# Attention and expert routing in one kernel: head pairs turned on VectorE, score buffers as a ring at the start, a changed load order at the seam

## The chip, the cores and the metric

The kernel runs on one core of a Trainium2 chip. Its time is the device time in microseconds (us) of one execution; lower is better. The engines of the core work side by side, each on its own list of instructions: TensorE (PE: matrix products and transposes, results in PSUM), VectorE (DVE), ScalarE (ACT), GpSimd (POOL) and SyncE (SP), which only issues transfers (DMA). SBUF is the working memory, PSUM the small memory of 8 banks that PE writes to.

## The reference

Attention over 4 batches, 12 heads, 448 tokens of 64 values, then a mixture of 8 experts, one expert for each of the 1792 tokens:

```
scores = cap * tanh((q @ k.T) / sqrt(64) / cap)
attn   = exp(scores - rowmax);  attn /= attn.sum(-1) + 1e-9
x      = (attn @ v), heads side by side           # 1792 x 768
logits = x @ w_gate;  e = argmax(logits)
gate   = softmax(logits)[e];  eom = sigmoid(x @ w_output_gate)[e]
out    = gate * eom * (relu(x @ w1[e]) @ w2[e])   # only the chosen expert
```

## The kernel before

**Units.** A unit is one batch and two heads (p and p + 6); there are 24 (6 for each batch), numbered u. The main loop does for each u on PE: the scores (`qk`, 4 tiles: three of two PSUM banks, one of one bank, each the sum of three products of a high and a low part of q and k), then `pv` of the unit before (8 products, result `u`), and every second unit the sums of the exponentials (`sums`). ACT takes the tanh of each score tile (PSUM to SBUF, `pt`) and one exp over the whole unit. POOL adds the exponentials up for the sums (`presum`, tile `pb`). DVE makes the planes of q and k: it turns the raw tile (`turned`: 32x32 blocks, which come out right because the load has put the blocks in place), casts it to the high part and subtracts for the low part (`planes_of`). Units 0 to 2 load q and k in natural order and PE turns them (`nat_k`, `nat_q`).

**k's planes** are 512 columns: 384 keys of both heads, and 128 columns where each head has its last 64 keys and zeros in the other head's half. DVE writes the first 384 with one operation and the two blocks of 64x64 with two more, for the high and again for the low part; the zeros are set once at the start.

**Score buffers.** PSUM has one bank `t` (all turning by DVE), one bank `sm`, and the pool `ps_s`: A and B (two banks each), C and D (one each). In units 0 to 2 the tiles go A, B, A, C; tile three of a unit waits until ACT has read tile one.

**Work for the router**, for each batch while the next one's units run, is hung into slots of the loop (`at`, slots f, g, h, q, e of a unit, in this order; x = 0 is the second unit of the next batch): reciprocals of the sums, then for each pair p the row `row_tr` (four PE transposes into a PSUM tile `trow`), `row_out` (DVE times the reciprocals, into one of three tiles `xr`) and a store into the token array `xs` in DRAM by SP; beside it the logits, the choice of an expert (`choose`: many small DVE operations), each token's place in the expert's table (`rank_mm`, `place`, `enter`) and a scatter into tables in DRAM by POOL (`scatter`).

**SP's list** is in program order: loads of k, q and v some units ahead, the stores of rows (`store_rows`, at a unit's end), at the seam the tables (`fetch_dma`, tile `tc`) and the weights (`load_raw`). Each of its transfers waits on the one eight places before it (eight semaphores taken in turn). `TURN` says how many planes are made before and after the middle of a unit; planes are made about three units ahead.

**The seam.** When the last unit's `pv` is done, the first expert block starts: POOL gathers 128 rows of `xs` by the table `tc` (`gather`), PE turns them (`tx`, tile `pt_x`), and the products with the weights follow (`php`, `py`). The expert part is the rest of the time.

Of the kernel before, what the change touches and what calls it, by code (L numbers as in the profile page):

```python
# [22 lines left out]
def tile_kernel(ctx: ExitStack, tc, q, k, v, cap, w_gate, w_ogate, w1, w2, out):  # L23
# [26 lines left out]
    for i, kind in enumerate((2, 4)):  # L50
# [8 lines left out]
    TURN = {0: (0, 0), 1: (0, 0), 3: (2, 1), 5: (2, 1), 6: (2, 1), 7: (2, 1), 9: (2, 1), 10: (1, 0), 11: (1, 0), 13: (2, 1),  # L59
            14: (2, 1), 15: (2, 1), 17: (1, 0), 20: (1, 0), 21: (0, 0), 22: (0, 0)}  # L60
# [22 lines left out]
    ps_s = att.enter_context(tc.tile_pool(name="ps_s", bufs=1, space=PSUM))  # L83
# [24 lines left out]
    def load_natural(dst, src, n, m, engs):  # L108
        for j in range(2):
            engs[j].dma_start(out=dst[:, 0:n, j], in_=src[j, 0:n * m].rearrange("(c p) d -> p c d", c=n))  # L110

    def load_nat(u, engs):
        (k0, q0), k_, q_ = nat[u], heads(k, u), heads(q, u)
        load_natural(k0, k_, NK, 128, engs)
        engs[1].dma_start(out=k0[0:64, NK], in_=k_[:, SK:S].rearrange("j p d -> p j d"))
        load_natural(q0, q_, NCH, CP, engs)

    def load_pair(src, u, tiles, to):
        t = raw1[tiles[u // 2 % 3]][:, 0:2 * S].rearrange("p (h r a) -> p h r a", h=2, a=32)
# [12 lines left out]

    def load_q(u):
        load_pair(q, u, (2, 3, 5), ldq)

    def v_main(u, eng):
        load_natural(vvs[u // 2 % 2][:, u % 2], heads(v, u), NK, 128, (eng, eng))

    def v_tails(u, eng):
        for j in range(2):  # L140
            h = j * NP + u % NP
            eng.dma_start(out=vvs[u // 2 % 2][64 * j:64 * j + 64, :, NK, j],
                          in_=v[u // NP, h:h + 2, SK:S].rearrange("h p d -> p h d"))
# [43 lines left out]
    for hl in kpl:  # L187
# [145 lines left out]
    def t_k(u):  # L333
        pl[u] = planes_of(k_parts(u, turned(ldk.pop(u), S)))
# [22 lines left out]

    def scores(name, z):
        return ps_s.tile([128, 2, 512], F32, tag="AB"[z], name=name)

    def single(name, z):
        return ps_s.tile([128, 512], F32, tag="CD"[z], name=name)
# [14 lines left out]
    def nat_q(u):  # L377
        pq = (scores("tq0", 1)[:, 0] if u == 2 else single("tq0", 1))[:, 0:S]
        for c in range(NCH):
            nc.tensor.transpose(pq[:, c * CP:(c + 1) * CP], nat[u][1][:, c].rearrange("p j d -> p (j d)"), ident[0:CP, 0:CP])  # L380
        return pq

    def qk(u, s):
        KH, KL, QH, QL = pl[u]
        if s == 0:
            pt[u] = ptp.tile([128, 2 * NK + 1, S], F32, tag="pt", name="pt")
        n = 2 if s < NK else 1
        sl = slice(s * 128, (s + 1) * 128)
        if s < NK:
            ps = scores("s", s % 2)  # L390
            for i, (x, y) in enumerate(((KH, QH), (KL, QH), (KH, QL))):
                for j in range(2):
                    h = slice(64 * j, 64 * j + 64)
                    nc.tensor.matmul(ps[:, j, 0:S], lhsT=x[h, sl], rhs=y[h], start=(i == 0), stop=(i == 2))  # L394
            ps = ps[:, :, 0:S]
        else:
            ps = single("s3", 0)[:, 0:S]
# [65 lines left out]
    def end_of_batch(b):  # L463
# [21 lines left out]
        def recips():  # L485
            r = T("rec", [CP, NCH, NP // 2, 4])
            nc.vector.tensor_scalar(out=r.rearrange("p c n j -> p c j n"), in0=rt["trec"][:, :, :, 0:NP // 2],
                                    scalar1=epsc[0:CP], scalar2=None, op0=ALU.add)
            nc.vector.reciprocal(out=r, in_=r)
            rec[b] = r.rearrange("p c n j -> p c (n j)")  # L490
# [24 lines left out]
        def gate_mul(g):  # L515
            if g == 0:
                T("gm", [CP, NCH, H, 16])
            for i in range(2):
                c = 2 * g + i
                nc.vector.tensor_tensor(  # L520
                    out=rt["gm"][:, c], in0=rt["pg"][:, i].rearrange("p (h e) -> p h e", h=H),
                    in1=rec[b][:, c].unsqueeze(2).to_broadcast([CP, H, 16]), op=ALU.mult)

        def logits():
            l = T("lg", [CP, NCH, 16])
# [3 lines left out]
            d = T("d")  # L529
            nc.vector.tensor_tensor(out=d, in0=l[:, :, 0:E], in1=mx.unsqueeze(2).to_broadcast(sh), op=ALU.subtract)  # L530

        def choose():

            d = rt["d"]
            cand = T("cand")
            stt(cand, d, 0.0, ALU.is_lt, iota8[0:CP], ALU.add)
            fi = T("fi", [CP, NCH])
# [4 lines left out]
            nc.vector.tensor_tensor(out=og, in0=ohb, in1=rt["lg"][:, :, E:2 * E], op=ALU.mult)  # L542
            den = T("den", [CP, 2, NCH])
            nc.vector.tensor_reduce(out=den[:, 1], in_=og, axis=AX.X, op=ALU.add)
# [15 lines left out]
        def place():  # L560
            ohb, ps = rt["ohb"], rt["ps"]
            rk = T("rk")
# [6 lines left out]
        def place2():  # L569
            rk = rt["rk"]  # L570
            nc.vector.tensor_tensor(out=rk, in0=rk, in1=rt["ohb"], op=ALU.mult)
            nc.vector.tensor_reduce(out=posi, in_=rk, axis=AX.X, op=ALU.max)

        def enter():

            den = rt["den"]
            nc.vector.tensor_reduce(out=den[:, 0], in_=rt["ex"], axis=AX.X, op=ALU.add)
            nc.vector.tensor_scalar(out=den[:, 1], in0=den[:, 1], scalar1=1.0, scalar2=None, op0=ALU.add)
            stt(den[:, 0], den[:, 0], 1e-9, ALU.add, den[:, 1], ALU.mult)
# [19 lines left out]
        def row_out(p):  # L599
            nrow[0] += 1  # L600
            x = xrp.tile([CP, NCH, 128], F32, tag=f"xr{nrow[0] % 3}", name="xr")
# [15 lines left out]

        L = lambda *fs: (lambda: [f() for f in fs])
        P = lambda f, *a: (lambda: f(*a))
        rws = [L(P(row_tr, p), P(row_out, p)) for p in range(NP)]  # L620
# [3 lines left out]
        if b < B - 2:  # L624
            at = {(-2, "q"): [g0], (0, "q"): [g1], (0, "e"): [sums_out], (1, "g"): [t[1]],
                  (2, "g"): [rws[0], rws[1]], (3, "g"): gts, (3, "h"): [logits], (4, "g"): [rws[2], rws[3]], (4, "h"): [choose],
                  (5, "g"): [rank_mm, place, rws[4]], (5, "h"): [place2, enter], (6, "g"): [rws[5]]}
            for i, x in enumerate(((6, "g"), (8, "g"), (9, "g"), (10, "g")) if b == 0 else ((6, "g"),) * NCH):
                at.setdefault(x, []).append(P(scatter, (i,)))
        elif b == B - 2:  # L630
# [6 lines left out]
                  (2, "g"): [rws[4], rws[5]], (2, "h"): [store_rows, P(load_v, NU - 2), *[nx] * 6, P(set_known, NE)],  # L637
                  (2, "q"): [lds[0], fd[0], lds[1], fd[1]],
# [342 lines left out]
    for u in range(NU):  # L981
        if u % 2 and u < NU - 3:
            load_v(u + 1)
        spare[0] = 0
# [386 lines left out]
```

## Time and the profile before

| | |
|---|---|
| median of 3 runs | 512.97 us (510.51 to 514.29) |
| profiled execution | 508.09 us, span 506.5 us |
| granted TensorE clock, mean | 0.996 |
| busy share PE, DVE, ACT, POOL | 96%, 76%, 73%, 57% |
| unit 3 (first with planes by DVE) begins on PE | 28.64 us |
| unit 8, unit 20 begin on PE | 63.88 us, 159.13 us |
| last full `pv` in the attention ends, first expert block begins on PE | 193.7 us, 197.62 us |

A window's row gives the busy time of each engine in it, then the granted clock, the busy share of the DMA engines and the rate; a timeline's row the start, the time from the first start to the last end of the merged instructions, the engine and line, and in brackets the engine's idle time before them and what ended it. PE's instructions overlap, so what a group costs PE is the distance to the start of the next one.

### The profile page before, as it was taken

To read this page: it belongs to the slowest core of one execution; us is meant where nothing else is said; L and a number is where in the kernel's file an instruction comes from. 1 tells how busy PE (TensorE), PEld (TensorE's weight loads), DVE (VectorE), ACT (ScalarE), POOL (GpSimd) and SP (SyncE) were. 2 spreads that over 40 slices of the span, in tenths; PEclk is the share of its full clock that TensorE was granted. 3 is DMA by queue.
4 is the path that set the end of the run, shared out by engine and by line. 5 is a ranking of instruction groups with operands and counts; after the bars stand their busy time and mean duration, and the time that the engine had idled before them with its cause. 6 is when DMAs were issued, how large, how long until landed. Compare 5 with 4: busy or idle time off the path is not lost. (4 is left out here: it accounts for less than half of the span.)

```text
span 506.5 us, 9980 instructions
## 1 busy us (share of the span) xinstructions
PE 487.3 (96%) x3064; PEld 338.1 (67%) x3064; DVE 385.3 (76%) x746; ACT 370.9 (73%) x433; POOL 290.8 (57%) x310
## 2 busy tenths in 40 slices
PE   7899999999999996999999999999999999999994
PEld 5444455444545442779988979978788867686691
DVE  5679899898998896898989869867677847565450
ACT  5899988889987794457588968867687856674551
POOL 7799998888998515575359682137363143622001
PEclk9999999999999999999999999999999999999998
DMA  7888868585531548873299245189689599790001
GB/s 174 138 151 143 143 120 148 96 148 97 83 70 38 106 122 305 273 240 116 96 384 363 72 146 207 32 289 349 224 305 379 204 396 404 200 380 33 1 33 50
DMA packets 152379, 91.92 MB, mean 181 GB/s; under 512 B 135026, under 2 KB 135162, under 8 KB 152320
## 3 DMA queue, kind: packets, MB, share of 16 engines
q1 hardware_dynamic: 142336, 58.24, 43.5%
q0 software_dynamic: 8832, 32.74, 17.6%
q8 instruction: 26, 0.43, 0.4%
q10 hardware_dynamic: 1152, 0.25, 0.2%
q14 instruction: 33, 0.27, 0.2%
HBM read 123.68 MB, written 12.04 MB: 268 GB/s over the span
## 5 line engine op out<-in xcount | busy, mean ns | idle before, releaser
L1074 DVE TENSOR_TENSOR wr<-raw,wr 128x768 fp32r<-128x768 f32 (+1 forms) x167 | 171.9, 1067 | 63.4 <-ACT wr L1073 62.0
L1073 ACT ACTIVATE wr<-raw 128x768 fp32r<-128x768 f32 (+1 forms) x167 | 150.4, 935 | 22.3 <-PE py L1095 10.3
L401 ACT ACTIVATE pt<-s,icap 128x896 f32<-128x896 f32 (+1 forms) x96 | 80.4, 916 | 12.9 <-PE s L394 12.2
L412 PE MATMUL u<-pt,vv 128*64 128x448 f32 x384 | 77.5, 545 | 0.3 <-ACT pt L404 0.3
L1095 PE MATMUL py<-wr,hh 128*128 128x384 f32 x352 | 77.3, 340 | 0.0
L1164 POOL DMA_INDIRECT out_dram<-yo,ti x13 | 20.2, 1555 | 98.7 <-ACT yo L1162 83.4
L1095 PE MATMUL php<-wr,xh 128*128 128x512 f32 x264 | 74.8, 404 | 0.0
L404 ACT ACTIVATE pt<-pt,capc 128x3136 f32<-128x3136 f32 x24 | 69.9, 2912 | 0.6
L1095 PEld LDWEIGHTS py<-wr,hh 128*128 128x128 f32 x352 | 61.2, 188 | 4.0 <-issue 3.7
L1095 PEld LDWEIGHTS php<-wr,xh 128*128 128x128 f32 x264 | 47.4, 188 | 12.8 <-issue 2.5
L412 PEld LDWEIGHTS u<-pt,vv 128*64 128x64 f32 x384 | 25.4, 136 | 39.3 <-issue 35.7
L420 POOL TENSOR_TENSOR pb<-pt 128x896 f32<-128x896 f32 x20 | 42.4, 2118 | 12.7 <-ACT pt L404 5.5
L425 POOL TENSOR_TENSOR pb<-pb,pt 64x448 f32<-64x448 f32 x40 | 45.6, 1139 | 3.1
L1095 PE MATMUL py<-wr,hl 128*128 128x384 f32 x176 | 44.8, 335 | 0.0
L421 POOL TENSOR_TENSOR pb<-pb,pt 128x896 f32<-128x896 f32 x20 | 42.0, 2102 | 1.6
L1095 PE MATMUL php<-wr,xl 128*128 128x512 f32 x132 | 41.5, 395 | 0.0
L1211 POOL DMA_DIRECT2D rh<-in_moe_w_dram x42 | 23.2, 555 | 15.8 <-DVE wr L1074 7.8
L1095 PEld LDWEIGHTS py<-wr,hl 128*128 128x128 f32 x176 | 31.8, 188 | 0.0
L1095 PEld LDWEIGHTS php<-wr,xl 128*128 128x128 f32 x132 | 24.7, 187 | 6.0
L290 DVE STREAM_TRANSPOSE tk<-raw 128x448 f32<-128x448 f32 x42 | 27.5, 655 | 0.9
L875 POOL DMA_INDIRECT xg<-xs,ti x14 | 19.3, 1381 | 6.1 <-POOL ti L868 3.7
L888 ACT ACTIVATE xh<-pt_x 128x512 fp32r<-128x512 f32 (+1 forms) x28 | 12.3, 487 | 13.3 <-PE pt_x L887 13.3
(315 smaller groups left out, 814.7 us busy)
## 6 DMA issues: line engine op xcount, KB each, us to landing
raw<-in_moe_w_dram SPq DMA_DIRECT2D x78, 512.0 KB
raw<-in_moe_w_dram SPq DMA_DIRECT2D x104, 384.0 KB
rh<-in_moe_w_dram POOLq DMA_DIRECT2D x18, 512.0 KB, 6.5
rh<-in_moe_w_dram POOLq DMA_DIRECT2D x24, 384.0 KB, 8.1
raw<-in_q_dram SPq DMA_DIRECT2D x45, 112.0 KB
vv<-in_v_dram SPq DMA_DIRECT2D x48, 96.0 KB
raw<-in_k_dram SPq DMA_DIRECT2D x40, 112.0 KB
xs<-xr SPq DMA_DIRECT2D x36, 112.0 KB
```

The costliest lines, as they stand in the source:

```text
L290: nc.vector.transpose(out=ps, in_=src.rearrange("p r a -> p (r a)"))
L401: nc.scalar.activation(out=pt[u][:, 2 * s:2 * s + n], in_=ps, func=ACTF.Tanh, scale=icap)
L404: nc.scalar.activation(out=pt[u], in_=pt[u], func=ACTF.Exp, scale=capc)
L412: nc.tensor.matmul(ups[u][64 * j:64 * j + 64], lhsT=V[:, c, j, :], rhs=P[:, 2 * c + (j if c < NK else 0)], start=(c == 0), stop=(c == NK))
L420: eng.tensor_tensor(out=s1[u], in0=P[:, 0:2], in1=P[:, 2:4], op=ALU.add)
L421: eng.tensor_tensor(out=s1[u], in0=s1[u], in1=P[:, 4:6], op=ALU.add)
L425: eng.tensor_tensor(out=s1[u][h, j], in0=s1[u][h, j], in1=P[h, 2 * NK], op=ALU.add)
L1073: nc.scalar.activation(out=t[:, 0, 0:F], in_=raw, func=ACTF.Copy)
L1074: nc.vector.tensor_tensor(out=t[:, 1, 0:F], in0=raw, in1=t[:, 0, 0:F].bitcast(F32), op=ALU.subtract)
L1095: nc.tensor.matmul(ps[g][:, 0:n], lhsT=st[:, c], rhs=w[:, z, g * n:(g + 1) * n], start=(c == 0 and st is hi and z == 0), stop=(c == (KD, K ...
L1164: nc.gpsimd.indirect_dma_start(out=out, out_offset=bass.IndirectOffsetOnAxis(ap=ti, axis=0), in_=y, in_offset=None, bounds_check=NT - 1, o ...
L1211: nc.gpsimd.dma_start(out=d, in_=rows_of(src, e, w, c), **kw)
```

## The change

**Rows of odd pairs.** For batches 0 and 1 the pairs 1, 3, 5 are no longer turned by PE: DVE turns the unit's result `ut` in blocks into PSUM (`row_v`, tile `tkr`), multiplies with reciprocals that it has turned the same way (`recips_b`, from the sums), and SP stores the row with four transfers of 32 partitions and 32 values each (128 bytes) where the two before had 64 values (256 bytes). The slots move: row 0 now follows the reciprocals in slot g of x = 1, rows 1, 3, 5 stand in slot e.

**Keys.** The zeros stand in the raw tile; a k tile is turned with two operations (384 and 128 columns), and the 512 columns are cast and subtracted at once. Each head's tile is loaded for itself: eight transfers for two units where there were four. Which 64 keys are a head's own differs between the two heads, so v's loads take other rows.

**Small tiles.** For batches 0 to 2 the logits, differences, indices, ranks and denominators stand in the bank `t` instead of SBUF; epsilon is added by ACT while it copies the sums; `gate_mul` does two blocks with one operation.

**Score buffers.** In units 0 to 2 the six banks are a ring of three tiles of two banks, for scores, natural q and `u`; unit 1's last tile takes `sm`. Before unit 3 the pool is opened again as A, B, C, D.

**Seam.** The first table is fetched before the last unit's v and before the first two weight tiles.

```diff
-    TURN = {0: (0, 0), 1: (0, 0), 3: (2, 1), 5: (2, 1), 6: (2, 1), 7: (2, 1), 9: (2, 1), 10: (1, 0), 11: (1, 0), 13: (2, 1),
-            14: (2, 1), 15: (2, 1), 17: (1, 0), 20: (1, 0), 21: (0, 0), 22: (0, 0)}
+    TURN = {0: (0, 0), 1: (0, 0), 3: (2, 1), 5: (2, 1), 6: (2, 1), 7: (2, 1), 13: (2, 1), 19: (2, 1),
+            20: (0, 0), 21: (0, 0), 22: (0, 0)}
...
+    def load_k(u):
+        t = kview[u // 2 % 3]
+        for i in range(u % 2, 2):
+            for c in range(4):
+                j, x = divmod(c, 2)
+                nc.sync.dma_start(
+                    out=t[32 * c:32 * c + 32, i, 2 * j:2 * j + 14],
+                    in_=blocks(k[u // NP, j * NP + u % NP + i - u % 2], x).rearrange("(r b) a -> b r a", b=32))
...
+    for t in kview:
+        nc.vector.memset(t[0:64, :, 14:16], 0.0)
+        nc.vector.memset(t[64:128, :, 0:2], 0.0)
...
     def turned(src, n):
         ps = tbank([128, n], "tk")
-        nc.vector.transpose(out=ps, in_=src.rearrange("p r a -> p (r a)"))
+        if n == S:
+            nc.vector.transpose(out=ps, in_=src.rearrange("p r a -> p (r a)"))
+        else:
+            nc.vector.transpose(out=ps[:, 0:SK], in_=src[:, 2:14].rearrange("p r a -> p (r a)"))
+            nc.vector.transpose(out=ps[:, SK:].rearrange("p (n k) -> p n k", n=2),
+                                in_=src.rearrange("p (n r) a -> p n (r a)", r=2)[:, 0::7])
...
     def scores(name, z):
-        return ps_s.tile([128, 2, 512], F32, tag="AB"[z], name=name)
+        ring[0] += 1
+        return ps_s[0].tile([128, 2, 512], F32, tag="AB"[z] if begun else f"r{ring[0] % 3}", name=name)
...
+    def fixed():
+        begin.close()
+        ps_s[0] = att.enter_context(tc.tile_pool(name="ps_s", reuse_waits="tile", bufs=1, space=PSUM))
...
             ssb = T("ssb", [128, S])
-            nc.scalar.activation(out=ssb, in_=smt.pop(b), func=ACTF.Copy)
+            nc.scalar.activation(out=ssb, in_=smt.pop(b), func=ACTF.Identity, bias=epsc)
...
-            rk = T("rk")
+            rk = rt["rk"] = small("rkb", sh) if b < B - 1 else T("rk")
...
+        def recips_b():
+            ps = tbank([128, S], "tks")
+            nc.vector.transpose(out=ps, in_=rt["ssb"])
...
+            for a in range(4):
+                g = 2 + a // 2
+                nc.vector.reciprocal(out=r[32 * a:32 * a + 32], in_=t[32 * g:32 * g + 32, 0:NP // 2])
+
+        def row_v(p):
+            nrow[0] += 1
+            ps = tbank([128, S], "tkr")
+            nc.vector.transpose(out=ps, in_=ut[b * NP + p])
+            x = xrp.tile([128, NCH * 128], F32, tag=f"xr{nrow[0] % 3}", name="xr")[:, 0:S].rearrange("p (t m) -> p t m", m=32)
+            nc.vector.tensor_tensor(out=x, in0=ps.rearrange("p (t m) -> p t m", m=32),
+                                    in1=rt["recb"][:, p // 2].unsqueeze(2).to_broadcast([128, NB, 32]), op=ALU.mult)
...
-            at = {(-2, "q"): [g0], (0, "q"): [g1], (0, "e"): [sums_out], (1, "g"): [t[1]],
-                  (2, "g"): [rws[0], rws[1]], (3, "g"): gts, (3, "h"): [logits], (4, "g"): [rws[2], rws[3]], (4, "h"): [choose],
-                  (5, "g"): [rank_mm, place, rws[4]], (5, "h"): [place2, enter], (6, "g"): [rws[5]]}
+            at = {(-2, "q"): [g0], (0, "q"): [g1], (0, "e"): [sums_out], (1, "g"): [t[1], rws[0]], (1, "e"): [recips_b],
+                  (2, "e"): [rws[1]], (3, "g"): gts, (3, "e"): [rws[3]], (4, "g"): [rws[2]], (4, "h"): [logits, choose],
+                  (5, "g"): [rank_mm, place, place2, rws[4]], (5, "h"): [enter], (6, "e"): [rws[5]]}
...
-                  (2, "g"): [rws[4], rws[5]], (2, "h"): [store_rows, P(load_v, NU - 2), *[nx] * 6, P(set_known, NE)],
-                  (2, "q"): [lds[0], fd[0], lds[1], fd[1]],
+                  (2, "g"): [rws[4], rws[5]], (2, "h"): [store_rows, P(v_main, NU - 2, nc.sync), P(v_tails, NU - 2, nc.sync), *[nx] * 6, P(set_known, NE)],
+                  (2, "q"): [fd[0], P(v_main, NU - 1, nc.sync), *lds[:2], fd[1]],
...
+        if u == NN:
+            fixed()
```

PE's list at the end of unit 9's scores (`s`), the rows of batch 0, `pv` (`u`) and the sums (`sm`), before:

```order
L394 MATMUL s<-QH,K4H 128x448 x2
L394 MATMUL s<-QH,K4L 128x448 x2
L394 MATMUL s<-QL,K4H 128x448 x2
L597 MATMUL trow<-ident,ut 112x128 x8
L412 MATMUL u<-pt,vv_120 64x448 x8
L444 MATMUL sm<-pb,ohc 32x448 x4
```

and now:

```order
L434 MATMUL s<-QH,K4H 128x448 x2
L434 MATMUL s<-QH,K4L 128x448 x2
L434 MATMUL s<-QL,K4H 128x448 x2
L452 MATMUL u<-pt,vv_120 64x448 x8
L484 MATMUL sm<-pb,ohc 32x448 x4
```

Eight transposes (rows 0 and 1) are gone here; row 0's four now stand one unit earlier, right behind the reciprocals' transposes `trec`. DVE's list in the same unit (planes of k, planes of q, rows), before:

```order
L290 STREAM_TRANSPOSE tk<-raw_0_106 128x448
L280 CAST K2H<-tk 128x384
L280 CAST K2H<-tk 64x64 x2
L286 TENSOR_TENSOR K2L<-tk,K2H 128x384
L286 TENSOR_TENSOR K2L<-tk,K2H 64x64 x2
L290 STREAM_TRANSPOSE tk<-raw_2_108 128x448
L280 CAST QH<-tk 128x448
L286 TENSOR_TENSOR QL<-tk,QH 128x448
L602 TENSOR_TENSOR xr<-trow,rec 112x512 x2
```

and now:

```order
L310 STREAM_TRANSPOSE tk<-raw_0_106 128x384
L311 STREAM_TRANSPOSE tk<-raw_0_106 128x128
L297 CAST K2H<-tk 128x512
L303 TENSOR_TENSOR K2L<-tk,K2H 128x512
L308 STREAM_TRANSPOSE tk<-raw_2_108 128x448
L297 CAST QH<-tk 128x448
L303 TENSOR_TENSOR QL<-tk,QH 128x448
L682 STREAM_TRANSPOSE tkr<-ut 128x448
L684 TENSOR_TENSOR xr<-tkr,recb 128x448
```

Six operations behind the turning of k (the small ones stand as x2) have become two of full width behind two turnings, and row 1 is two operations of DVE. SP's list at the seam (`vv`: v of the last two units; `tc<-tab`: pieces of the first table; `raw_0_106`: the first weight tile; TENSOR_LOAD: a number read into a register), before:

```order
L142 DMA vv_121<-in_v_dram 64x2x64 x2
L110 DMA vv_121<-in_v_dram 128x3x64 x2
L831 TENSOR_LOAD meta
L831 ISA x2
L837 ISA
L837 DMA raw_0_106<-in_moe_w_dram 128x1024
L857 TENSOR_LOAD meta
L857 ISA x2
L860 ISA
L860 DMA tc<-tab_102 128x2
```

and now:

```order
L938 DMA tc<-tab_104 128x2
L938 ISA
L938 DMA tc<-tab_105 128x2
L114 DMA vv_121<-in_v_dram 128x3x64 x2
L909 TENSOR_LOAD meta
L909 ISA x2
L915 ISA
L915 DMA raw_0_106<-in_moe_w_dram 128x1024
```

The table's four pieces (the last one stands here) have moved ahead of v's last load and of the weight tile.

## Rows read from the trace of the kernel before

**Rows 1.** Windows: stretch, length, busy us of each engine, clock, DMA share, GB/s
```profile
0.00:30.00 30.00, 24.68 (x170) 15.54 (x170) 18.65 (x88) 22.00 (x21) 22.85 (x46) 1.00 0.77 154
30.00:66.00 36.00, 36.00 (x226) 16.73 (x224) 32.34 (x73) 33.28 (x30) 33.99 (x21) 1.00 0.86 148
66.00:153.00 87.00, 86.67 (x556) 43.05 (x557) 79.64 (x186) 77.44 (x76) 77.02 (x50) 1.00 0.60 107
...
198.00:506.50 308.50, 300.48 (x1874) 243.50 (x1872) 217.43 (x305) 205.30 (x276) 131.99 (x172) 0.99 0.60 217
```

**Rows 2.** Waits of PE in 0:30: total us, times, longest
```profile
PE s L394 <- ACT pt L401: 2.7, 3, 1.7
```

**Rows 3.** Timeline of ACT in 10:200 (tanh L401, exp L404)
```profile
11.52 0.63 ACT L401 ACTIVATE pt<-s,icap 128x448 f32<-128x448 f32 x1 [0.47 <-PE s L399]
...
22.79 3.53 ACT L401 ACTIVATE pt<-s,icap 128x896 f32<-128x896 f32 x4 [1.35 <-PE s L394]
...
115.35 2.91 ACT L404 ACTIVATE pt<-pt,capc 128x3136 f32<-128x3136 f32 x1
...
122.02 2.91 ACT L404 ACTIVATE pt<-pt,capc 128x3136 f32<-128x3136 f32 x1
```

**Rows 4.** Timeline of PE, units 9, 12, 19 and 20
```profile
73.98 1.08 PE L597 MATMUL trow<-ident,ut 128*112 128x128 f32 x8
74.99 3.23 PE L412 MATMUL u<-pt,vv 128*64 128x448 f32 x16
...
98.44 0.65 PE L597 MATMUL trow<-ident,ut 128*112 128x128 f32 x4
99.02 3.23 PE L412 MATMUL u<-pt,vv 128*64 128x448 f32 x16
...
154.74 0.65 PE L482 MATMUL trec<-ident,ssb 128*112 128x128 f32 x4 [0.50 <-ACT ssb L477]
...
167.68 0.65 PE L597 MATMUL trow<-ident,ut 128*112 128x128 f32 x4 [0.65 <-DVE xr L602]
```

**Rows 5.** Groups of DVE in 0:215: count, busy us, mean ns, idle before
```profile
L290 DVE STREAM_TRANSPOSE tk<-raw 128x448 f32<-128x448 f32 x42 | 27.5, 655 | 0.9
L602 DVE TENSOR_TENSOR xr<-trow,rec 112x512 f32<-112x512 f32 x21 | 14.0, 686 | 3.9 <-PE trow L597 1.9 <-DMA xs<-xr 1.3 <-PE trk L551 0.4
...
L578 DVE TENSOR_SCALAR den<-den 112x4 f32<-112x4 f32 x3 | 2.9, 962 | 0.0
...
L280 DVE CAST K1H<-tk 128x384 fp32r<-128x384 f32 x5 | 2.8, 558 | 2.1 <-PE tk L374 2.0
...
L280 DVE CAST K0H<-tk 64x64 fp32r<-64x64 f32 x10 | 2.2, 217 | 0.1
...
L571 DVE TENSOR_TENSOR rk<-rk,ohb 112x32 f32<-112x32 f32 x3 | 2.0, 651 | 0.0
```

**Rows 6.** Timeline of SP's issues, start
```profile
12.12 2.05 SPq L124 DMA_DIRECT2D raw<-in_k_dram  x4
14.22 3.21 SPq L124 DMA_DIRECT2D raw<-in_q_dram  x4
17.47 2.63 SPq L124 DMA_DIRECT2D raw<-in_k_dram  x4
...
57.73 1.02 SPq L110 DMA_DIRECT2D vv<-in_v_dram  x2
```

**Rows 7.** Timelines of SP, POOL and PE at the seam
```profile
179.15 1.30 SPq L142 DMA_DIRECT2D vv<-in_v_dram  x2
...
182.69 0.37 SPq L837 DMA_DIRECT2D raw<-in_moe_w_dram  x1
183.94 2.09 SPq L860 DMA_DIRECT2D tc<-tab  x4
...
190.47 1.14 POOL L875 DMA_INDIRECT xg<-xs,ti  x1 [0.70 <-DMA tc<-tab]
...
197.62 0.87 PE L887 MATMUL pt_x<-ident,xg 128*128 128x128 f32 x6 [3.90 <-DMA xg<-xs,ti]
```

More of the change, by code (lines that the diff above doesn't have):

```diff
@@ L333, in t_k @@
     def t_k(u):
-        pl[u] = planes_of(k_parts(u, turned(ldk.pop(u), S)))
+        pl[u] = planes_of(k_parts(u, turned(ldk.pop(u), SK + 128)))
     def t_q(u):
@@ L356, in turn_next @@
         del turns[:n]
+    ring = [0]
     def scores(name, z):
-        return ps_s.tile([128, 2, 512], F32, tag="AB"[z], name=name)
+        ring[0] += 1
+        return ps_s[0].tile([128, 2, 512], F32, tag="AB"[z] if begun else f"r{ring[0] % 3}", name=name)
+    ready = {}
     def single(name, z):
-        return ps_s.tile([128, 512], F32, tag="CD"[z], name=name)
+        if not begun:
+            return scores(name, z)[:, 0]
+        return ready.pop(z, None) or ps_s[0].tile([128, 512], F32, tag="CD"[z], name=name)
+    begun = []
+    def fixed():
+        begin.close()
+        ps_s[0] = att.enter_context(tc.tile_pool(name="ps_s", reuse_waits="tile", bufs=1, space=PSUM))
+        begun.append(1)
+        for z in (1, 0):
+            ready[z] = ps_s[0].tile([128, 512], F32, tag="CD"[z], name=("s3", "u")[z])
     spare = [0]
@@ L486, in recips @@
             r = T("rec", [CP, NCH, NP // 2, 4])
-            nc.vector.tensor_scalar(out=r.rearrange("p c n j -> p c j n"), in0=rt["trec"][:, :, :, 0:NP // 2],
-                                    scalar1=epsc[0:CP], scalar2=None, op0=ALU.add)
-            nc.vector.reciprocal(out=r, in_=r)
+            nc.vector.reciprocal(out=r.rearrange("p c n j -> p c j n"), in_=rt["trec"][:, :, :, 0:NP // 2])
             rec[b] = r.rearrange("p c n j -> p c (n j)")
@@ L517, in gate_mul, with small @@
                 T("gm", [CP, NCH, H, 16])
[L518 to L522, printed above, removed]
-        def logits():
-            l = T("lg", [CP, NCH, 16])
+            cs = slice(2 * g, 2 * g + 2)
+            nc.vector.tensor_tensor(
+                out=rt["gm"][:, cs], in0=rt["pg"].rearrange("p i (h e) -> p i h e", h=H),
+                in1=rec[b][:, cs].unsqueeze(3).to_broadcast([CP, 2, H, 16]), op=ALU.mult)
+        def small(nm, shape):
+            n = math.prod(shape[1:])
+            return tbank([CP, n], nm).rearrange("p (c e) -> p c e", c=shape[1])
+        def logits():
+            if b < B - 1:
+                w = rt["lgd"] = small("lgd", [CP, NCH, 16 + E + 1])
+                l, d = w[:, :, 0:16], w[:, :, 16:16 + E]
+            else:
+                l, d = T("lg", [CP, NCH, 16]), T("d")
             nc.vector.tensor_reduce(out=l, in_=rt["gm"].rearrange("p c h e -> p c e h"), axis=AX.X, op=ALU.add)
@@ L576, in enter @@
             den = rt["den"]
-            nc.vector.tensor_reduce(out=den[:, 0], in_=rt["ex"], axis=AX.X, op=ALU.add)
-            nc.vector.tensor_scalar(out=den[:, 1], in0=den[:, 1], scalar1=1.0, scalar2=None, op0=ALU.add)
-            stt(den[:, 0], den[:, 0], 1e-9, ALU.add, den[:, 1], ALU.mult)
+            x = small("dex", [CP, 1, NCH])[:, 0] if b < B - 1 else den[:, 0]
+            nc.vector.tensor_reduce(out=x, in_=rt["ex"], axis=AX.X, op=ALU.add)
+            nc.vector.tensor_scalar(out=x, in0=x, scalar1=1e-9, scalar2=None, op0=ALU.add)
+            stt(den[:, 0], den[:, 1], 1.0, ALU.add, x, ALU.mult)
             nc.vector.reciprocal(out=ent[:, b, :, 1], in_=den[:, 0])
@@ L616, in row_out, with store @@
                 stores.append(store)
+        NB = S // 32
+        BYV = range(1, NP, 2) if b < B - 2 else ()
+        def recips_b():
+            ps = tbank([128, S], "tks")
+            nc.vector.transpose(out=ps, in_=rt["ssb"])
+            r = T("recb", [128, NP // 2, NB])
+            t = ps.rearrange("p (t r) -> p r t", r=32)
+            for a in range(4):
[8 more added lines that the diff above has]
+                                    in1=rt["recb"][:, p // 2].unsqueeze(2).to_broadcast([128, NB, 32]), op=ALU.mult)
+            def store():
+                for a in range(4):
+                    m0 = D * (p + a // 2 * NP) + 32 * (a % 2)
+                    nc.sync.dma_start(
+                        out=xs[b * S:(b + 1) * S, m0:m0 + 32].rearrange("(t i) m -> i t m", i=32),
+                        in_=x[32 * a:32 * a + 32])
+            stores.append(store)
         L = lambda *fs: (lambda: [f() for f in fs])
         P = lambda f, *a: (lambda: f(*a))
-        rws = [L(P(row_tr, p), P(row_out, p)) for p in range(NP)]
+        rws = [P(row_v, p) if p in BYV else L(P(row_tr, p), P(row_out, p)) for p in range(NP)]
         t = [sums_out, L(sums_tr, recips), L(P(gate_mm, 0), P(gate_out, 0)), L(P(gate_mm, 1), P(gate_out, 1))]
```

65 lines of the change are left out of this document (38 added, 27 removed).

## The prediction

> **What bounds the kernel now.** I read the windows first [rows 1]. In the first 30 us PE is busy 24.7 of 30, and from 30 on it has hardly a gap: 86.67 of 87 us between 66 and 153, 300.5 of 308.5 after 198. ACT, DVE and POOL have 77.4, 79.6 and 77.0 of the same 87 us, and the clock is full throughout. So what counts is PE's list, and the few places where PE waits. Then I read PE's waits: at the start 2.7 us in three pieces for ACT, because tile three of a unit needs the buffer of tile one [rows 2]; ACT itself stands still twice there, 0.47 and 1.35 us, for scores that PE could not write [rows 3]. In the middle PE waits for nothing but a row's copy in unit 20, 0.65 us, and the copied sums in unit 19, 0.50 us [rows 4]. At the seam it waits 3.90 us for the gathered rows [rows 7]. The expert part is PE's own and the change does not touch it.
>
> The sum is made against the profiled execution, 508.1 us (span 506.5), which is 4.9 us under the median of the runs shown, 513.0; I move the median by the same amount. One per cent, 5.1 us, is about what a measurement of this kernel can tell from no change.
>
> **Rows of odd pairs.** Eight transposes cost PE 1.01 us (73.98 to 74.99), four cost 0.58 (98.44 to 99.02) [rows 4]. A batch's rows stood as 8, 8, 4 and 4: 3.2 us; now as three times four: 1.7. Batch 0 gains 1.5. In batch 1 the last four stood in unit 19 just ahead of `trec`, which waits for ACT all the same: that wait grows from 0.50 to 1.1 us, so batch 1 gains 0.9. Together **-2.4 us**, all on PE's path.
>
> DVE takes the work over: an odd row is a turning (655 ns as for k) and a product of 448 columns (some 620, from 686 for 512 columns) in place of 686: +0.59 us, six times 3.5. The turned reciprocals are 655 and four small operations at about 217, twice: 3.0. Keys: 655 + 2 x 558 + 4 x 217 = 2.64 us a unit before [rows 5]; now two turnings and two operations at 690. The second turning does not stand in the trace: it costs between nothing (only the columns count, 0.655 for both) and a whole one (1.31); I take a fixed part plus 64 columns as the casts of 384 and 64 columns show it, together 217 ns: 2.25 us a unit, so -0.39, 21 times -8.2 (ends: -12.7 and +1.1). The small tiles: a number of 112x4 takes 962 ns and a product of 112x32 651, where a 64x64 cast takes 217 [rows 5]; these two alone give 1.2 a batch, three times 3.5. In all DVE has about 5 us less, not more (ends -10 and +4), and it had 7 us free in the 87 [rows 1]. I cost the rest of DVE's edits (reciprocals straight from PSUM, `gate_mul` in one, fewer memsets) at nothing, since DVE's free time covers them; without that cover they would be under 1 us.
>
> In unit 20 PE waits 0.65 us because DVE comes late to row 1, after the ranks and denominators. If those two operations take 217 ns there instead of 651 and 962, DVE is 1.2 us earlier and the wait goes: **-0.6**. [...]
>
> **Score buffers.** With three double buffers tile three no longer waits, and unit 2's scores start before ACT has run dry. What PE can win is its 2.7 us [rows 2]. ACT then sets the start: its instructions stand one behind the other but for 0.47 + 1.35 = 1.8 us [rows 3]. So unit 3 begins between 1.8 and 2.7 us earlier, if v of unit 2 is there. It stands on SP behind k of units 4 and 5, now eight transfers where 2.63 us were spent on four; at 0.51 each (2.05 for four of that form) that is 1.5 us later [rows 6]. I take **-1.9**, and keep 0 and -2.7 as ends.
>
> **Loads.** Ten pairs of units load k with eight transfers, and six rows are stored with four instead of two. Whatever is behind them on SP is later: v of units 8 and 9, issued from 57.73, has five such pairs ahead, 5 x (8 x 0.51 - 2.6) = 7.4 us. It is used at 74.99; with 6.0 us to land (the gather of rows 7: 191.6 to 197.6, the longest I have) the lead is 11.3, and 9.4 once PE is 1.9 earlier. Covered: **0**.
>
> **Seam.** In the list before, v's last load, a register read and a weight tile stood between v's 64-row load (over at 180.45) and the table (183.94); the register read alone takes the 0.88 from 183.06. Now the table follows at 180.45 + 0.9 = 181.4, 2.5 us earlier, and with it the gather (190.47) [rows 7]. The gather also leaves before most of the weights and not among them, so it may land sooner than in 6.0 us. What is late next is the first weight tile, 2.5 us later, on which DVE's first split waits. Ends 0 and -3.9; I take **-3.0**.
>
> **Pace.** With rows gone, units without a row come down to what ACT needs for one: exp to exp 6.67 us in unit 14 [rows 3]. I add **+0.3** for short waits of that kind. ACT's spare 9.6 us and POOL's 10.0 in the 87 [rows 1] are four times what PE loses there, so neither becomes the bound.
>
> **Sum.** -2.4 - 0.6 - 1.9 - 3.0 + 0.3 = -7.6: the profile 500.5, the median 505.4. With all ends on one side it is -9.6 or -2.1.
>
> **Rivals.**
> 1. *The stall at the seam stays* (508.4 = 505.4 + 3.0). The gather still meets weights in the DMA engines, or the table is no longer what is late, but a store of rows or DVE's split. For it: 6.0 us for a gather says that it queues behind something, and everything ahead of it comes earlier too. Against it: the table alone is 2.5 us up.
> 2. *The start gives nothing* (507.3). v of unit 2 comes late, or ACT's list holds PE back a unit later. For it: SP is issuing without a pause there. Against it: all three pieces of PE's wait end with a buffer that came free, and now a third one stands ready.
> 3. *SP's list becomes the bound; slower.* In units 8 to 11 `pv` waits for v and DVE for k, because a half-size load costs SP as much as a whole one: each transfer waits on the one eight before it. q's four loads of that form took 3.21, 0.80 each [rows 6]. At 0.80 a pair costs 6.4 instead of 2.6, six pairs until unit 11 make 22.8 against a lead of 9.4: PE waits 13.4, and the median is 518.8. It decides from 0.68 us a load on (6 x (8c - 2.6) = 9.4 + 7.6). Against it: the DMA engines were busy 0.86 of that stretch [rows 1], so q's loads waited for bytes, and halves carry half. [...]
> 4. *The change does not do what it says*: DVE's small operations stay as slow in PSUM, or the turning with a gap costs far more. DVE then has up to 4 us more of its 7 spare: no change to the median but the 0.6.
>
> **Chances.** Forecast (with rival 4 in it, which leaves it by under 1 us) 0.66, its own range 502.5 to 507.5; rival 1 0.14; rival 2 0.10; rival 3 0.10. Faster by over 1% means under 507.8: 0.64 of the first, 0.06 each of rivals 1 and 2: 0.76. Slower by over 1%, from 518.1 on: rival 3 at its full price, 0.06 of its 0.10. Within 1%: the rest, 0.18. The range is 501 to 511: it holds the forecast's case, rivals 1 and 2 and what lies between, and leaves out rival 3 and a gain with every end on the good side.
>
> **What the profile after would show.** Unit 3 begins on PE at about 26.7 instead of 28.64, and PE's wait on ACT in the first 30 us is under 1 us. 24 fewer `trow` transposes; unit 20 begins 4 us or so earlier than 159.13. No DVE operation of the choice of batches 0 to 2 above 300 ns. The wait of `pt_x` for its gather is about 1 us, with the table issued before v's last load. SP: k's eight loads in 4.1 us. I am wrong if `pv` or DVE wait for transfers between 60 and 100 us, if the wait at the seam is as long as before, or if PE's gaps on ACT in the middle add up to more than 1 us.

## The result and the profile after

The changed kernel takes **499.5 us** (median of 6 runs, 498.72 to 501.27) against 512.4 (6 runs, 510.51 to 514.29): ratio 0.9754, interval 0.9725 to 0.9783, 12.9 us less. Forecast was 505.4 with a range from 501 to 511: the direction was right, the time is below the range. From profile to profile the gain was only 6.8 us (span 506.5 to 499.7), close to the sum of the steps, 7.6; the medians gained almost twice that. Ratios, their intervals (95%, in brackets) and the figures on the clock below leave out runs more than 1.5% above the fastest of their kernel, counted as slow; medians hold all runs.

The windows of the changed kernel (stretch, length, busy us of PE, PEld, DVE, ACT and POOL, clock, DMA share, GB/s) answer to [rows 1]:

```profile
0.00:30.00 30.00, 27.03 (x187) 17.23 (x189) 21.56 (x88) 24.31 (x25) 24.18 (x46) 1.00 0.72 144
30.00:66.00 36.00, 36.00 (x229) 16.89 (x227) 31.32 (x53) 33.36 (x29) 34.37 (x22) 1.00 0.76 129
66.00:153.00 87.00, 85.28 (x543) 41.61 (x541) 78.91 (x160) 78.46 (x76) 79.46 (x53) 1.00 0.68 119
198.00:499.70 301.70, 292.24 (x1825) 238.57 (x1823) 210.84 (x295) 197.93 (x266) 133.40 (x165) 0.99 0.59 215
```

PE is busy 27.03 of the first 30 us instead of 24.68. Its waits there (total us, times, longest) no longer hold a score tile's buffer, where [rows 2] had 2.7 us:

```profile
PE wps L178 <- DVE wz L168: 1.2, 1, 1.2
PE s L434 <- DVE QH L297: 0.8, 1, 0.8
PE tq L420 <- DMA raw<-in_q_dram: 0.6, 1, 0.6
PE s L434 <- ACT QH L295: 0.2, 1, 0.2
```

PE's timeline in units 19 and 20 answers to [rows 4]: `trec` waits 1.17 us (forecast 1.1). The wait for a copied row in unit 20 has not gone as forecast: the 0.65 us of [rows 4] have become 0.35, and the next scores wait another 0.35 for the row after it.

```profile
149.72 0.65 PE L522 MATMUL trec<-ident,ssb 128*112 128x128 f32 x4 [1.17 <-ACT ssb L517]
...
162.38 0.65 PE L646 MATMUL trow<-ident,ut 128*112 128x128 f32 x4 [0.35 <-DVE xr L651]
...
164.18 0.47 PE L434 MATMUL s<-QH,K1H 64*128 64x448 f32 x2 [0.35 <-DVE xr L651]
```

DVE's groups in 0:215 (count, busy us, mean ns, idle before) answer to [rows 5]. A k tile costs 592 + 327 + 2 x 692 = 2303 ns (forecast 2250), an odd row 656 + 625 = 1281 (1275), the turned reciprocals 421 each (217). Rank and denominator fell from 651 and 962 ns to 191 and 170:

```profile
L310 DVE STREAM_TRANSPOSE tk<-raw 128x384 f32<-128x384 f32 x21 | 12.4, 592 | 0.5
...
L311 DVE STREAM_TRANSPOSE tk<-raw 128x128 f32<-128x128 f32 x21 | 6.9, 327 | 0.7
...
L682 DVE STREAM_TRANSPOSE tkr<-ut 128x448 f32<-128x448 f32 x6 | 3.9, 656 | 0.1
L684 DVE TENSOR_TENSOR xr<-tkr,recb 128x448 f32<-128x448 f32 x6 | 3.8, 625 | 0.2
...
L677 DVE RECIPROCAL recb<-tks 32x42 f32<-32x42 f32 x8 | 3.4, 421 | 0.1
...
L303 DVE TENSOR_TENSOR K1L<-tk,K1H 128x512 fp32r<-128x512 f32 x4 | 2.8, 692 | 0.1
...
L619 DVE TENSOR_TENSOR rk<-rkb,ohb 112x32 f32<-112x32 f32 x3 | 0.6, 191 | 0.1
...
L627 DVE TENSOR_SCALAR dex<-dex 112x4 f32<-112x4 f32 x3 | 0.5, 170 | 0.1
```

At the seam, POOL's gather starts at 182.26 instead of 190.47 [rows 7], and PE's `pt_x` follows the last `pv` with no wait (timelines of POOL and PE):

```profile
182.26 1.21 POOL L953 DMA_INDIRECT xg<-xs,ti  x1 [0.34 <-POOL ti L946]
```
```profile
188.72 1.15 PE L965 MATMUL pt_x<-ident,xg 128*128 128x128 f32 x6
```

The signs came: unit 3 begins at 25.56 us (26.7 forecast), unit 20 begins 5.0 us earlier (4), and the wait for the gather is gone (1 us forecast). So the steps show in the profile, but for the wait in unit 20. What they do not show is why ordinary runs gained twice as much; that is what the experiments are about.

### The profile page after: what moved, and what is told of

It reads as the page before. It is cut to its first block, busy times and chain, and to the rows that moved or that the text cites. A ratio compares the mean times of both kernels' runs of the same rounds, so it can differ in the third digit from the quotient of the medians.

```text
span 499.7 us, 9942 instructions
## 1 busy us (share of the span) xinstructions
PE 484.3 (97%) x3040; PEld 335.9 (67%) x3040; DVE 380.4 (76%) x688; ACT 370.0 (74%) x433; POOL 296.0 (59%) x310
## 5 line engine op out<-in xcount | busy, mean ns | idle before, releaser
L441 ACT ACTIVATE pt<-s,icap 128x896 f32<-128x896 f32 (+1 forms) x95 | 79.4, 917 | 9.2 <-PE s L434 8.2
L1175 PEld LDWEIGHTS php<-wr,xh 128*128 128x128 f32 x264 | 47.4, 188 | 12.8 <-issue 2.8
L1345 POOL DMA_INDIRECT out_dram<-yh,toh x6 | 7.8, 1300 | 34.9 <-ACT wr L1153 16.7
L637 POOL DMA_INDIRECT tab<-ent,posi x16 | 16.4, 1024 | 9.2 <-DVE ent L629 4.8
## 6 DMA issues: line engine op xcount, KB each, us to landing
raw<-in_moe_w_dram SPq DMA_DIRECT2D x78, 512.0 KB
rh<-in_moe_w_dram POOLq DMA_DIRECT2D x18, 512.0 KB, 8.0
```

The costliest lines, as they stand in the source:

```text
L1175: nc.tensor.matmul(ps[g][:, 0:n], lhsT=st[:, c], rhs=w[:, z, g * n:(g + 1) * n], start=(c == 0 and st is hi and z == 0), stop=(c == (KD, K ...
```

## The experiments

They were timed in four groups of four kernels, each group on one chip together with the kernel before, whose medians there were 510.3, 512.5, 512.6 and 512.0 us. Ratios are to the kernel before ("before" for short) on the same chip.

### The kernel before, again

No edit. 

> The kernel before, unchanged, once more with its trace. Question: its profiled execution had a span of 506.5 us, while its timed runs had a median of 512.4, so ordinary runs lose some 4 us that its profile does not show. Theory (the seam): the wait of the first pt_x for the gathered rows, 3.90 us in the first profile, is a matter of how the gather meets the weights and is longer in ordinary runs; a second profiled execution with a span of 510 or so then shows 7 to 8 us there and the same start (unit 3 at 28.6). Rival (the first profiled execution was fast in many small places, or at the start): the second has the wait at 3.9 again and the rest spread or at the start. Ratio 1.000 by both.

Measured: 1.0022 (0.9993 to 1.005), as it should be. Its profiled execution (the second profile of before) had a span of 509.4 us and a mean clock of 0.987 (0.996 in the first profile). Unit 3 begins at 30.89 us instead of 28.64, and the wait for the gather was shorter, 2.89 us. The seam theory falls. The timeline of PE at unit 1 shows what happened instead; the first row is that of the first profile:

```profile
16.05 0.47 PE L394 MATMUL s<-QH,K1H 64*128 64x448 f32 x2 [1.72 <-ACT pt L401]
...
13.66 0.36 PE L394 MATMUL s<-QL,K1H 64*128 64x448 f32 x2
15.75 0.74 PE L394 MATMUL s<-QH,K1H 64*128 64x448 f32 x2 [1.73 <-ACT pt L401]
16.29 0.58 PE L394 MATMUL s<-QH,K1L 64*128 64x448 f32 x2
```

The wait is the same 1.7 us, but behind it two products of the same form take 0.74 us, not 0.47. The windows of this execution (PE's busy time, clock, DMA share, GB/s):

```profile
14.00:16.00 2.00, 0.28 (x4) 0.68 0.70 115
16.00:22.00 6.00, 6.00 (x23) 0.54 0.81 128
194.00:198.50 4.50, 1.96 (x12) 1.00 0.97 358
198.50:202.50 4.00, 3.65 (x14) 0.57 1.01 354
```

and of the first profile of before:

```profile
14.00:16.00 2.00, 0.33 (x4) 1.00 0.78 127
16.00:22.00 6.00, 5.95 (x35) 1.00 0.77 122
194.00:198.50 4.50, 0.88 (x9) 1.00 0.97 332
198.50:202.50 4.00, 4.00 (x21) 1.00 0.91 307
```

With each of PE's two long waits the granted clock falls to 0.50 and stays there for some 6.5 and 3.5 us (from 15.0 and 199.0 on; 0.54 and 0.57 are the means of the windows), with 23 instructions from 16 to 22 us where there were 35, and then returns to 1.00. The first profile happened to be an execution in which it did not fall: there the waits of 1.72 and 3.90 us left it at 1.00. Of 70 executions of before on the four chips, 5 had a mean clock of 0.996 or more, with a median span of 505.8 us (507.4 us as a time); the 24 from 0.986 to 0.988 had 510.4. The slope of span over mean clock is 427 us for a whole unit (correlation -0.80): 0.008 less clock is 3.4 us more. The six runs of the changed kernel all lie between 0.995 and 0.997.

So this kernel, with PE busy for 96% of the first profile's span, loses time to half clock too (0.50 after waits of 1.73 and 2.89 us in the second), and the rows of the first show that not every such wait is followed by it.

### Parts alone

The seam's load order alone:

```diff
-  (2, "h"): [store_rows, P(load_v, NU - 2), ...]
-  (2, "q"): [lds[0], fd[0], lds[1], fd[1]],
+  (2, "h"): [store_rows, P(v_main, NU - 2, nc.sync), P(v_tails, NU - 2, nc.sync), ...]
+  (2, "q"): [fd[0], P(v_main, NU - 1, nc.sync), *lds[:2], fd[1]],
```

> The kernel before with the new load order at the seam alone. By the prediction's term (3.0 us, ends 0 and 3.9) the median falls from 512.4 to 509.4; by the theory that ordinary runs wait longer than 3.9 us for the gather it falls by 7 to 8, to about 505. By the rival that the seam's stall merely changes its cause it stays at 512.

Measured: 507.7 us, 0.9953 (0.9927 to 0.998), 2.6 us less on this chip, near the prediction's 3.0; the 7 to 8 are refuted. In its profile the wait is gone and the clock behind the seam full (1.00), but half clock (0.50 from 16.5 to 19.5 us) stands behind the start's wait of 1.7 us.

The score buffers alone (`fixed`, `scores`, `single`, `nat_q` and the call before unit 3, as in the change):

```diff
+        if u == NN:
+            fixed()
```

> The kernel before with the three double score buffers in units 0 to 2 alone. The prediction's term was 1.9 us (ends 0 and 2.7); the profile of the changed kernel shows unit 3 at 25.56 instead of 28.64, 3.1 us earlier. So the median is 510.5 by the prediction's step and 509.3 by the profile. If the ordinary runs of before lose their 4 us at the start (rival to the seam theory), it falls by 6 or more, to 506.

Measured: 506.6 us, 0.992 (0.9894 to 0.9946), 3.7 less, twice the prediction's 1.9. Unit 3 begins at 25.19, 3.45 us before the first profile's and 5.7 before the second's, and the clock in the first 30 us is full (1.00). But its wait at the seam is now 4.8 us, with half clock behind it (0.59 from 195 to 198.5 us).

The keys alone (`load_k`, `turned`, `k_parts`, zeros, v's rows):

```diff
+        if u >= NN:
+            return [hi, lo], [(hi, lo, ps)]
```

> The kernel before with the change to the keys alone (zeros in the raw tiles, eight loads a pair instead of four, two turnings and two casts instead of one and six). The prediction costs it at 0 on PE's path: DVE gets some 8 us of work off, of which only the 0.65 us in unit 20 can show, so 511.8 to 512.4. If twice as many transfers on SP hold up v (the prediction's rival 3), the median rises by 2 or more; if DVE is what ordinary runs of before wait for, it falls by 2 or more.

Measured: 512.35, 1.0019 (0.9983 to 1.0055): nothing that can be told from zero, as the prediction's step has it. The medians stand 2.1 us apart, the mark set for late loads of v, but the interval of the ratio holds 1, and in the profile no product of the attention waits for v.

Buffers and seam together (both edits above):

> The kernel before with both the three score buffers and the seam's order, and nothing else of the change. Theory (waits and the clock behind them): 3.3 us at the start and 3.9 at the seam off the 507.7 that before takes at full clock, so 500.5, with a mean clock of 0.995 or more in every run; what is left to the 499.5 of the whole change is the rows' 1.9 us, less what is lost later. Prediction's steps (1.9 and 3.0, clock left alone): 510.3 - 4.9 = 505.4. Sum of the two parts measured alone, ring -3.7 and seam -2.6: 504.0.

Measured: 503.1 us, 0.9834 (0.979 to 0.9877), 8.5 of the 12.5 us of the whole change, mean clocks 0.995 to 0.998 in all six runs. The clock came as expected, the time 2.5 us later than the theory's figure; the sum of the two parts, 6.3, is less than both together. At full clock its runs still spread from 501.4 to 505.8 us, so the clock is not all that differs between executions.

### Work in the waits

Nothing is taken away; idle products are added in front of the two waiting instructions:

```diff
+    fill = [20]
...
+            for _ in range(fill.pop() if fill else 0):
+                nc.tensor.transpose(ps[:, 0], ident, ident)
...
+            if u == 1 and s == 2:
+                warm(21)
             qk(u, s)
```

> The kernel before with work for TensorE in two of its waits: 21 small bf16 products (0.08 us each, 1.7 us) ahead of unit 1's third score tile, and 20 transposes (0.14 each, 2.8 us) ahead of the first pt_x; nothing reads their results. Nothing is taken away, so a theory that counts waits alone (the rival) expects 510.3 us as before, or a little more. Theory (the clock): in the second profile of before the granted clock stood at 0.50 for 7 us behind the first wait and for 3.5 us behind the one at the seam, and in the first profile it did not; a filled wait leaves the clock at 1.00, each 0.50 behind a wait costs half its length, and the median goes to that of the executions whose mean clock is 0.996, about 507.7, with mean clocks of 0.995 or more in nearly all runs.

Measured: **507.2 us, 0.9908 (0.9876 to 0.994): 5.3 us less for 41 useless instructions**, mean clocks 0.995 to 0.998 in all nine runs. Its windows:

```profile
14.00:16.00 2.00, 1.73 (x27) 1.00 0.73 119
16.00:18.50 2.50, 2.33 (x15) 1.00 0.50 80
18.50:22.00 3.50, 3.50 (x20) 1.00 1.07 170
194.00:198.50 4.50, 4.50 (x37) 1.00 0.94 347
```

A theory that counts waits alone cannot give this. The two halves apart:

> The kernel before with the 21 small products in unit 1's wait alone (the seam's wait is left empty). Filling both waits took 5.3 us off. By the second profile of before, half clock lasted 7 us behind this wait and cost unit 3 2.25 us; so 2.2 to 3.5 us less than before, and a mean clock of about 0.992. Rival: the clock would have fallen at the seam alone, and this filling gives nothing.

> The kernel before with the 20 transposes in the seam's wait alone. Half clock lasted 3.5 us there, 1.6 us lost; so 1.5 to 2 us less than before, and a mean clock of about 0.991. With the filled start it should make up the 5.3 us of both; if both alone give less than 4 together, something else in the filled kernel was faster.

Measured: the start alone 506.1 us, 0.9905 (0.9871 to 0.994); the seam alone 511.0, 0.9998 (0.997 to 1.0025). So nearly all of it comes with the start, 5.9 us where 3.5 were expected at most, and nothing that can be told from zero with the seam, where 1.5 to 2 were expected. The filled start has mean clocks of 0.997 or 0.998 in six of seven runs, and by the slope above that is worth some 3 us; the rest is not the clock alone. In its profile the later wait for the gather is only 0.81 us and the clock is full (1.00) behind it too. The filled seam has mean clocks of 0.985 to 0.996; its profile is its one run at 0.996, with full clock (1.00) at the unfilled start, whose wait is 1.7 us. Why the gather came sooner once the start was filled is not shown.

### The whole change without one part

Rows back on PE (`TURN` and the row steps in their places of before):

```diff
-        BYV = range(1, NP, 2) if b < B - 2 else ()
+        BYV = ()
```

> The whole change but for the odd pairs' rows, which go back to TensorE (with the row steps and the turns of k and q in the places of before). The prediction's term is 2.4 us, so 499.5 + 2.4 = 501.9; the two profiles give 1.9 between unit 3 and unit 23's exp, so 501.4. Rival: VectorE's rows are paid for elsewhere (its list, twice the stores) and the time stays at 499.5 or falls.

Measured: 504.1 us, 0.9854 (0.9815 to 0.9893), 5 us more than the whole change by the ratios, twice what was expected. Its profile is its slowest run, 507.0 us. From unit 3 to unit 23's exp (the middle) it takes 159.48 us (the whole change 156.46 in its second profile), and at 196.8 the first expert products wait for DVE's split of the weights, and behind that four of them take 1.96 us (at 198.38) where four took 1.19 (at 193.17); the whole change has no such wait:

```profile
196.83 0.73 PE L1175 MATMUL php<-wr,xl 128*128 128x512 f32 x2 [2.47 <-DVE wr L1154]
```

Small tiles back in SBUF (the hunks on `gate_mul`, `logits`, `choose`, `place` and `enter` undone):

```diff
-            rk = rt["rk"] = small("rkb", sh) if b < B - 1 else T("rk")
+            rk = T("rk")
```

> The whole change but for choice's small tiles, which stay in SBUF in all batches. By the prediction they take VectorE 3.5 us of work in three batches, off TensorE's path but for 0.6 us at unit 20's row: 499.5 to 500.1. Rival: VectorE is late without them and holds up rows and planes, 501.5 or more.

Measured: 505.0 us, 0.9872 (0.9834 to 0.991), nearly 6 us more than the whole change: the rival. PE's longest waits in the middle (total, times, longest):

```profile
PE trk L588 <- DVE ohb L578: 2.0, 1, 2.0
PE s L434 <- DVE rk L605: 1.9, 1, 1.9
PE trow L635 <- DVE xr L640: 1.6, 1, 1.6
```

The middle takes 161.39 us, 1.9 more than with the rows on PE on the same chip (159.50, buffers and seam alone): in these two profiles, giving DVE the rows without the small tiles makes the middle slower.

Keys as before (the hunks of the keys undone):

```diff
-        if u >= NN:
-            return [hi, lo], [(hi, lo, ps)]
```

> The whole change but for the keys (zeros written into the planes again, four loads a pair, one turning and six casts a unit). The prediction costs the keys' part at 0 on TensorE's path: 499.5, at most 0.6 more. Rival (VectorE has no room for its rows without the 8 us that the keys gave back): TensorE waits for rows and planes as in the kernel without the small tiles, 501.5 to 505.

Measured: 503.4 us, 0.9825 (0.9802 to 0.9848), 3.5 us more. The rival again: the middle takes 159.20 us, 2.27 of it a gap of PE in unit 21, for which the profile names no releaser; beside it DVE's rows wait 1.44 and 0.90 us for stores to land.

The seam's order as before (the diff of the seam above, reversed):

> The whole change but for the load order at the seam, which is that of before. Prediction's step: 3.0 us more than the whole change, 502.5. Theory (wait and clock): the wait for the gather is back, 4 to 5 us as in the kernel with the score buffers alone (4.8), and half clock for some 3.5 us behind it in most runs, 1.7 more: 505 to 506, with a mean clock of 0.992 or so.

Measured: 505.0 us, 0.9843 (0.9819 to 0.9867), 5.1 more than the whole change beside it, against the 3.0 of the prediction. PE's timeline and windows there show wait and clock together:

```profile
193.96 1.54 PE L965 MATMUL pt_x<-ident,xg 128*128 128x128 f32 x6 [5.85 <-DMA xg<-xs,ti]
```
```profile
194.00:198.00 4.00, 4.00 (x14) 0.50 0.88 295
```

### The whole change again, and two attempts at its last wait

> The whole change, unchanged, beside the parts on one chip. The clock theory expects a mean clock of 0.995 or more in every run, since no wait of TensorE over 1.3 us is left, and 499.5 us again. The first profile lost 2.1 us behind the seam (303.6 us from the first pt_x to TensorE's last product, 301.4 before; 1.3 of it a wait on ACT behind late weights at 400 us): if that is how one execution fell, the second profile has 302 or less there; if it belongs to the change, 303 or more again.

Measured: 499.9 us, 0.9757 (0.9736 to 0.9778); in the last group, on another chip, 499.3, 0.9753; 11 runs with mean clocks from 0.995 to 0.998. The stretch behind the seam took 301.64 us: the 2.1 us that the first profile lost there were that execution's own.

Batch 0's and 1's sums behind `pv`:

```diff
-  ..., (1, "g"): [t[1], rws[0]], (1, "e"): [recips_b],
+  ..., (1, "q"): [t[1], rws[0]], (1, "e"): [recips_b],
```

> The whole change, with the turning of the sums (trec) and row 0 moved behind the unit's pv products, so that unit 19 no longer waits 1.17 us for ACT's copy of the sums. If TensorE's waits in the middle are on the path, 498.4 us against 499.5 of the whole change on the same chip; rival (the reciprocals now come late for the gates, or VectorE's list slips): the same or more.

Measured: 499.4, 0.9743 (0.9721 to 0.9764), the same, and the wait still 1.2 us: it belongs to batch 2's sums, whose steps stand in another table. The run says nothing about the question. Batch 2's then, with the whole change once more beside it:

```diff
-  (0, "f"): [P(sums, EARLY), g1, sums_out], (0, "h"): [t[1], *gts, logits, choose],
+  (0, "f"): [P(sums, EARLY), g1, sums_out], (0, "q"): [t[1], *gts, logits, choose],
```

> The whole change, with batch 2's turning of the sums, gates, logits and choice moved behind unit 19's pv products: this is the wait of 1.17 us that the move of the other batches' sums did not reach. If it is on TensorE's path: 1.0 to 1.2 us less than the whole change, 498.5 to 498.9. Rival: the choice now comes 3.2 us later on VectorE, trk waits for it in unit 20, and nothing is won.

> The whole change once more, as the measure for the kernel with the later gates on the same chip: 499.5 to 499.9, mean clock 0.995 or more in every run.

Measured: 502.3 us, 0.9804 (0.9775 to 0.9834), 3.0 more than the whole change beside it: worse than even the rival. The 1.17 us are gone, but DVE is now late for unit 20's rows, and in the profile the clock falls behind that, to 0.54 on average. PE's rows and window:

```profile
160.80 0.65 PE L646 MATMUL trow<-ident,ut 128*112 128x128 f32 x4 [0.77 <-DVE xr L651]
161.66 0.62 PE L646 MATMUL trow<-ident,ut 128*112 128x128 f32 x4 [0.21 <-DVE rkb L614]
163.42 1.10 PE L646 MATMUL trow<-ident,ut 128*112 128x128 f32 x4 [1.14 <-DVE xr L651]
```
```profile
162.50:170.00 7.50, 6.58 (x25) 0.54 0.73 132
```

No version tried is faster than the whole change.

## Why the prediction was wrong, step by step

| stretch, us | before, first profile | before, second | change, first | change, second |
|---|---|---|---|---|
| to unit 3 | 28.64 | 30.89 | 25.56 | 25.36 |
| to unit 23's exp (on ACT) | 158.90 | 158.88 | 157.04 | 156.46 |
| to the first `pt_x` | 10.08 | 9.08 | 6.12 | 6.12 |
| to the end of PE's last product | 301.44 | 303.01 | 303.54 | 301.64 |
| to the end | 7.44 | 7.54 | 7.44 | 7.02 |
| span | 506.5 | 509.4 | 499.7 | 496.6 |

**The step that failed is "I move the median by the same amount."** The profile summed against was an execution at full clock, and "the clock is full throughout" was true of it and of few others. The change takes away both waits with which the clock fell to 0.50 in the second profile of before, so an ordinary run gains the waits and the clock. The five executions of before at full clock have a median of 507.4 us: the change is 7.9 us under them, near the 7.6 of the sum, and the other 5.0 of the 12.9 are what before loses in ordinary runs. The 4.9 us between profile and median stood in the prediction as a constant; they were in the main a cost of the very waits that it removed (filling them with idle products gave 5.3 back).

Part of the agreement is luck. The first profiles differ by 6.8 us because 8.9 were gained up to the first `pt_x` and 2.1 lost behind it in that one execution. The second profiles differ by 12.8, as the medians do, but that of the change is the fastest of its five runs.

**Score buffers** (1.9 forecast): 3.1 to 3.4 in waits, a term sized too small. I took ACT's idle 1.8 us for the bound; PE's own 2.7 us of waits all went, and some small ones with them. With the clock, 5.5.

**Seam** (3.0): the wait went whole, 4.0 us in the first profile, and what I kept back for "what is late next" did not come. Undoing it costs 5.1 with the clock.

**Rows** (2.4, less 0.3 for short waits): 1.9 and 2.6 from unit 3 to unit 20 in the two pairs of profiles, as forecast. Undoing them costs 5, so in the whole change they are worth more than their transposes.

**Wait in unit 20** (0.6): this term failed. The rank and the denominator, 1.06 and 0.96 us there in before, took 0.19 and 0.17, but PE still waited 0.35 and 0.35 us for copied rows, the second of which had waited 0.52 us for a store to land. From unit 20's first scores to unit 21's `pv` it took 13.42 us before and 13.50 after.

**DVE's edits at nothing**: right for the keys in the kernel before (no difference that can be told), wrong as a statement about the change. The prediction set DVE's work against 7 us free in a stretch of 87, and by that rival 4 had "no change to the median but the 0.6" if the small operations stayed slow. That failed: the rows fit on DVE only because keys and small tiles have made room, and undoing one of the two costs 3.5 or nearly 6. Free time in a stretch does not cover a row that PE needs at one moment. Together the sum of 0 hid that. The small tiles were also mis-sized: five operations of a batch came from 707, 702, 520, 651 and 962 ns to under 200 each, 7 us in three batches with one copy added; the prediction had counted two of them, 3.5. With the tiles back in SBUF, `rk` alone took 1.47 us in unit 20.

**Loads on SP** at 0: right. Eight loads took 4.08 to 4.45 us (forecast 4.1) in most places, 5.5 to 6.4 in three, and `pv` never waited for them. Rivals 1 to 3 did not occur, nor rival 4's slow operations. One reading against rival 3 was wrong: the DMA share of 0.86 is that of 30 to 66 us, while the four loads of 3.21 us were issued at 14.22, where it was 0.77.

## What to carry to other kernels

A wait of TensorE can cost more than its own length: of 11 waits of 1.7 to 5.9 us at the start and the seam in the profiles here, seven came with some 3 to 7 us at a granted clock of 0.50 and an eighth with slower products (four in 1.96 us instead of 1.19), and three left it at 1.00. Of three waits of 1.9 to 2.3 us in the middle, one was followed by products of the usual 0.36 and 0.47 us (keys as before), and the execution with the other two (small tiles back in SBUF) had a mean clock of 0.995, no lower than the whole change's. So a change that removes one can be worth more than the row of waits says; look at the granted clock behind every such wait, and in more than one execution. One profile is one execution: where it lies below all runs timed beside it, as here by 2.4 us, find out in what it is unusual before summing against it. Several edits that each give an engine room are costed together, not one by one.

## What the runs showed of the hardware

**Idle work paid.** 41 products that nobody reads made this kernel 5.3 us faster (ratio 0.9908, 0.9876 to 0.994).

**Small DVE operations on SBUF that began during one of GpSimd's additions ended just behind it; with an operand in PSUM they did not wait.** In the kernel before, `d`, `cand`, `ohb`, `og` and `rk` (two operands in SBUF) and `den` (one operand and constants) took 0.16 to 1.18 us for the same work; the reductions of the same tiles (one operand) took 186 to 187 ns. The trace shows when. Twelve of these operations began while one of GpSimd's additions (`pb`, on tiles in SBUF) ran; each of them ended 0.03 to 0.05 us behind the end of that addition. The other sixteen began while none ran, and took 0.16 to 0.20 us. Rows of before, batch 1 beside additions and batch 2 beside scatters:

```profile
136.65 2.10 POOL L421 TENSOR_TENSOR pb<-pb,pt 128x896 f32<-128x896 f32 x1
137.80 0.99 DVE L667 SCALAR_TENSOR_TENSOR cand<-d,iota 112x32 f32<-112x32 f32 x1
138.82 2.35 POOL L425 TENSOR_TENSOR pb<-pb,pt 64x448 f32<-64x448 f32 x2
140.04 1.18 DVE L542 TENSOR_TENSOR og<-ohb,lg 112x32 f32<-112x32 bf16 x1
...
158.79 0.96 POOL L588 DMA_INDIRECT tab<-ent,posi  x1 [0.30 <-PE u L412]
159.46 0.19 DVE L667 SCALAR_TENSOR_TENSOR cand<-d,iota 112x32 f32<-112x32 f32 x1
```

With an operand in PSUM the same operation is short while an addition runs, 0.18 us in the changed kernel; the 17 of its operations on the new tiles that began during an addition took 0.16 to 0.20 us:

```profile
90.16 2.12 POOL L460 TENSOR_TENSOR pb<-pt 128x896 f32<-128x896 f32 x1 [0.77 <-PE sm L484]
90.76 0.18 DVE L745 SCALAR_TENSOR_TENSOR cand<-lgd,iota 112x32 f32<-112x32 f32 x1
```

Why they wait is not shown by these rows. The prediction had counted on 217 ns in PSUM for two of them, and had not named the additions.
